# The signal's second stage on sums and differences of mirrored samples: a gated mix of a long convolution and an MLP

## The chip, the core and the metric

The kernel runs on one core of a Trainium2 chip. TensorE (PE) multiplies matrices, VectorE (DVE), ScalarE (ACT) and GpSimd (POOL) work on tiles in on-chip memory, SyncE (SP) mostly issues DMAs; ScalarE and GpSimd issue some too. Each engine runs its own instructions strictly in order and waits on semaphores for the others. The metric is the device time of one execution in microseconds (us). Everything is float32 (or fp32r, the same width).

## The reference

Rows of a signal u (2048 samples, 512 channels) are convolved with a kernel that a state-space model of 128 states gives for each channel; the same rows go through an MLP (512 to 1792 to 512, gelu); a gate per row mixes the two.

```python
P = exp(logdA[:, :, None] * l[None, None, :])       # 512 x 128 x 2048
K = einsum("dn,dnl,dn->dl", Cc, P, dB).real         # taps
y = irfft(rfft(pad(u)) * rfft(pad(K)))[:L] + u * Dskip
b = gelu(x @ w1 + b1) @ w2 + b2                     # x is u
g = sigmoid((x * gate_w).sum(-1))
out = g * y + (1 - g) * b
```

## The kernel before

Two functions follow one another: `front` and `conv`.

`front` computes the MLP, the taps K and the first stage of both Fourier transforms. Its work is cut into tasks by four streams (dense, taps, signal, early); each task has an engine, a hold (its modelled duration), a due time and dependencies, and the planner (`Plan.run`) gives out, engine by engine, the ready task with the earliest due time. The due times come from the constants at the file's head (T_, D_, W_). So these numbers set the order of every engine's instructions in the front. TensorE has three kinds of matmuls there: the hidden layer (ph, L917 to L919), the output layer (acc, L962 to L964) and the taps (pk, L726).

The transform of 4096 points is cut into two stages. In the **first stage** (`first_stage`, L428 to L442) 16 blocks of the signal (xl, 128 x 512 each, 256 KB) are multiplied, in four groups of 32 rows, with a small matrix c1t, two blocks (ux[0], ux[1]) per step, in eight steps; SP loads the blocks (L452), ScalarE copies the result out (L456), and SP stores it to memory (tu_d, L459). The stream `early` (L481) loads 27 of the 32 rows of tu_d again, 256 KB each, into the tiles den, attic and loft (`us[n]`). The taps go the same way: their first stage is stored to tk_d (L767).

MLP results are stored to `out` in memory and added to there: ScalarE copies acc into the tile io (L983), and GpSimd issues an accumulating store (L1006). The last two of these wait for `look` (L1014), a copy of one element on GpSimd that reads a tile xh after the last step of the hidden layer has written it (L937), so that all earlier traffic is through.

`conv` is written out by hand. It goes over 16 steps s of two rows each (n = 2s, 2s + 1), and in a step come:

- `fetch` of rows of tk_d for later steps (SP, L1129); the first N_TK = 8 are fetched ahead of the loop, with the matrices c2 (`consts`, L1121, 192 KB, cc) after every second one, four in all. The other matrices come at s = 2, 4, 6, 8. cc has four buffers in turn, tk has N_TK. Rows 16 to 23 go to t3 instead, at s = 0
- at s = 4, 5 and 6, loads of the five rows of tu_d that had no room in the front (SP, L1274)
- `product(s)`: six VectorE operations (L1174 to L1179) on the signal's spectrum (ur, ui in PSUM) and the taps' (kr, ki)
- `signal(s + 1)` and `taps(s + 2)`: the second stage (`pair`, L1152): for c = 0, 1 (real and imaginary part) and i = 0, 1 a matmul of a 128 x 64 matrix with a row tile of 128 x 512. For c = 0 the matrix is cut from cc (f), for c = 1 it is f1, whose halves are swapped and one negated (`matrices`: GpSimd for the first two, L1137 and L1138, ScalarE for the others, L1140 and L1141). ScalarE copies the taps' result out (L1160)
- `inverse(s)`: four matmuls with 64 x 64 matrices (pa, L1191), ScalarE copies (sa, L1197), SP stores to t_d (L1199); after each group of eight rows they are loaded again, turned, into t3 and den (`turn`, L1214). From s = 7 the MLP's results are loaded (L1228)

The profile counts a float32 matmul as two instructions: four matmuls of a group are x8. After the loop come `rest` (the last output-layer matmuls, L1245 to L1247), the last stage (pb, L1316), the gate and the stores (L1336).

Of the kernel before, what the change touches and what calls it, by code (L numbers as in the profile page):

```python
# [32 lines left out]
NB = 2 * NSB  # L33
T_0 = 28.031
T_MLP = 402.005
K_0 = 34.529
T_KG = 347.257
U_0 = 23
U_GAP = 18
LAG = 13.166  # L40
TABLE = 30.571
D_KA = -21.02
D_KP = -70.174
D_S1 = -64.005
D_EV = -0.687
D_H = -44.182
D_LO = -26.872
# [8 lines left out]
T_EARLY, T_LOFT, T_DEN = 434.731, 499.385, 583.061
Y_K, Y_U = 40.448, 33.741
W_MLP = (-0.0424, -0.0295, 0.0137)
W_KG = (-0.0358, -0.0266, -0.0229)
W_U = (-0.0255, -0.1355, -0.0209)  # L60
D_MAG = -1.089
D_ROT = 0.621
D_CON = -2.254
D_PHA = 0.57
D_PRE = -1.138
D_XL = 26
D_COE = -4.808
D_OUT = -10.383
D_DTB = -996.723
D_D0A = -269.982  # L70
D_LAST = -1.103
N_REST = 3
D_KA0 = 35
D_DT = 5
D_PRM = -94
D_D0 = 0
D_WAVE0 = -333.922
D_COE0 = -195.511
D_SP1 = -346.272
D_G0 = 14  # L80
D_GW = 568.694
D_XS0 = 115.71
T_PRE = 23
W_CAST = (0, 1, 0, 0, 1, 0, 1, 0, 1, 1, 0, 1, 0, 0)
X_CAST = (1, 1, 1, 1)
D_X0, D_B2, D_B2A, D_DM = -480, 20, -11.213, -79.268
N_G = 9

N_ATTIC, N_LOFT, N_TK = 11, 8, 8
ASIDE = (4, 6, 13, 14)  # L90
# [3 lines left out]
N_ROOM = N_ATTIC + N_LOFT  # L94
N_US = N_DEN + N_ROOM

# [35 lines left out]
def constants():  # L132


    def om(e4):
        a = 2.0 * np.pi * (np.asarray(e4) % (4 * L)) / (4 * L)
        return np.cos(a), -np.sin(a)

    k0 = np.arange(32)
    p = np.arange(32)  # L140
    q = np.asarray(slot_q())
    k1 = np.arange(64)
    m = np.arange(32)

    er, ei = om(4 * (64 * np.outer(p, k0) + 16 * p[:, None]))

    c1 = np.tile(np.stack([er, ei], 2).reshape(32, 64), (4, 1))


    ko = np.asarray(k0_order())  # L150
    turn = 2.0 * np.pi * (ko[:, None] + 0.25) / 32
    half = 2.0 * np.pi * (ko[:, None] + 0.25) / 64
    g1 = np.zeros((P, 2, 2, 32))
    for b in range(2):
        up, down = turn * (p - 1), turn * p
# [155 lines left out]
def gated_mix(  # L311
# [25 lines left out]
    tu_d = dr.tile([32, P, D], F32, name="tu_d")  # L337
    tk_d = dr.tile([32, P, D], F32, name="tk_d")

# [5 lines left out]
    gate = cp.tile([P, 2, 16], F32, name="gate")  # L345
    c1t = cp.tile([P, 64], F32, name="c1t")

    def places(attic, loft, den):

        rooms = [attic[:, k] for k in range(N_ATTIC)] + [loft[:, k * D : k * D + D] for k in range(N_LOFT)]  # L350
        return [den[:, k] for k in range(N_DEN)] + rooms + rooms[: 32 - N_US]

    def front(pool, psum, keep, attic, loft, den):

# [72 lines left out]

        def first_stage(xs, due, evac, ahead=2):  # L428

# [4 lines left out]
            def products():  # L434
                for r, (bank, _) in enumerate(banks):
                    rs = slice(32 * r, 32 * r + 32)
                    for m, (x, _) in enumerate(xs):
                        nc.tensor.matmul(bank[64 * m : 64 * m + 64], c1t[rs], x[rs], start=True, stop=True)  # L438

# [6 lines left out]
        def signal():  # L446
            for s in range(8):
# [3 lines left out]
                for m in range(2):  # L451
                    move(256, lambda m=m, s=s: nc.sync.dma_start(ux[m], xl[2 * s + m]), t - 10, [], [("ux", m)])  # L452

                def evac(r, pp, key, s=s, t=t):
                    k = take("st", N_ST)
                    act(512, lambda: nc.scalar.copy(st[k], pp), t + D_EV, [key], [("st", k)])  # L456
                    for m in range(2):
                        move(
                            128, lambda m=m: nc.sync.dma_start(rows[:, 8 * s + 4 * m + r], st[k][64 * m : 64 * m + 64]),  # L459
                            t, [("st", k)], [("u_d", 8 * s + 4 * m + r)], out=True,  # L460
                        )

                first_stage(xs, t, evac)
            yield None

        def early():

            us = places(attic, loft, den)
            keys = [("ux", 0)] + [("st", k) for k in range(N_ST)]
            keys = [*keys, *(("ld", k) for k in range(N_LD)), "gwb"]  # L470
            yield 1e6
            for n in range(N_US):
                m = n - N_DEN
                if m < 0:
                    due, key = T_DEN + n, [("xc", n // 4)]
                elif m < N_ATTIC:
                    due, key = T_EARLY + 2.5 * m, [keys[m]]
                else:
                    due, key = T_LOFT + m, ["xt", "xv"] if m < N_ATTIC + 4 else ["tt"]
                move(  # L480
# [235 lines left out]
        def contract(u, c, k, t):  # L716
# [382 lines left out]
        while heap:  # L1099
# [10 lines left out]
    def conv(pool, ps, late, attic, loft, den):  # L1110
# [4 lines left out]
        us = places(attic, loft, den)  # L1115
        ko = k0_order()
# [7 lines left out]
        def fetch(n):  # L1124
            if 16 <= n < 24:
                t2s[n] = t3[:, n]
            else:
                t2s[n] = pool.tile([P, D], F32, tag="tk", name=f"tk{n}", bufs=N_TK)
            nc.sync.dma_start(t2s[n], tk_d[ko[n]])  # L1129

        def matrices(m):
# [3 lines left out]
            f1 = pool.tile([P, 4, 64], F32, tag="f1", name=f"f1{m}", bufs=2)  # L1135
            if m < 2:
                nc.gpsimd.tensor_scalar(f1[0:64], f[64:128], -1.0, None, ALU.mult)  # L1137
                nc.gpsimd.tensor_copy(f1[64:128], f[0:64])  # L1138
            else:
                nc.scalar.mul(f1[0:64], f[64:128], -1.0)  # L1140
                nc.scalar.copy(f1[64:128], f[0:64])  # L1141
            mats[m] = (f, f1), cc[:, 256:384].rearrange("p (s k) -> p s k", s=2)
# [3 lines left out]
        def pair(s, r, c, out):  # L1146

            for i in range(2):
                n = 2 * s + i
                w = mats[n // 4][0][c][:, n % 4]  # L1150
                x = t2s[n] if r else us[n]
                nc.tensor.matmul(out[64 * i : 64 * i + 64], w, x, start=True, stop=True)  # L1152
# [110 lines left out]
        for s in range(16):  # L1263
# [92 lines left out]

# [65 lines left out]
```

## Time and profile before

| | us |
|---|---|
| three runs | 507.9, 507.18, 507.18 (median 507.18) |
| the profiled execution: its span | 506.3 |
| last hidden-layer matmul of the front begins | 398.03 |
| conv's first matmul begins | 398.24 |
| inverse(0) begins | 408.91 |
| pb begins (the last stage) | 487.04 |
| last VectorE operation begins | 501.05 |

The times are those of the runs; the profiled execution is another one, and all points inside it are counted from the start of its span. Differences are made against that span.

A group row reads: line, engine, operation, output<-input, shapes, count | busy us, mean ns of one | idle time of the engine just before, and what ended it. A row of a timeline or of the chain begins with its start and its duration in us. The chain is followed back from the last instruction: at each point stands what released the work that came next. `SPq` is SP's queue of issues.

### The profile page before, as it was taken

How to read it: one execution, taken by the hardware profiler on the slowest of the kernel's cores; microseconds unless marked ns; L12 is line 12 of the kernel's file. 1: busy time of each engine (PE TensorE's matmuls, PEld its weight loads, DVE VectorE, ACT ScalarE, POOL GpSimd, SP SyncE). 2: the span in 40 equal slices, each digit the busy share in tenths (PEclk: the TensorE clock that was granted, in tenths of full speed). 3: DMA queues.
4: the chain of work that ended last, by engine and by line, in shares of the span. 5: the costliest groups of instructions: out<-in, count | busy, mean ns of one | idle time of the engine just before them, and what ended most of it. 6: DMA issues, size and time to landing. Idle time of an engine off the chain costs nothing.

```text
span 506.3 us, 12185 instructions
## 1 busy us (share of the span) xinstructions
PE 494.8 (98%) x4798; PEld 380.3 (75%) x4798; DVE 429.0 (85%) x794; ACT 347.2 (69%) x625; POOL 53.5 (11%) x93
## 2 busy tenths in 40 slices
PE   7999999999999999999999999999999999999995
PEld 7886988998889889889789878989889722222551
DVE  6999999998999999999899989999921188877544
ACT  4898757699683889968487997657643445568513
POOL 1001010101002011011110012001010300020003
PEclk9999999999999999999999999999999999999998
DMA  8958896416788545889850276984588997999998
GB/s 288 381 178 235 298 296 219 84 65 200 182 239 222 156 147 126 262 187 238 201 128 2 84 167 156 208 266 104 189 208 180 282 390 266 336 374 382 320 321 312
DMA packets 82680, 112.32 MB, mean 222 GB/s; under 512 B 39644, under 2 KB 41184, under 8 KB 82080
## 3 DMA queue, kind: packets, MB, share of 16 engines
q1 hardware_dynamic: 74704, 87.06, 53.7%
q0 software_dynamic: 7264, 21.73, 18.3%
q10 hardware_dynamic: 656, 2.75, 1.7%
q8 instruction: 38, 0.62, 0.5%
q14 instruction: 18, 0.15, 0.1%
HBM read 61.71 MB, written 49.81 MB: 220 GB/s over the span
## 4 chain that ended last, share of the span: by engine, by line
PE 70%; DVE 13%; DMA 7%; ACT 4%; SPq 2%; issue 2%; DVEq 0%; ACTq 0%
PE pk L726 10%; PE acc L962 7%; PE ph L917 7%; PE ph L919 7%; PE ph L918 7%; PE acc L964 7%; PE acc L963 6%; PE p2u L1152 5%; PE p2k L1152 4%; PE pa L1191 3%; PE pb L1316 3%; DMA tk<-tk_d 2%; PE ph L438 2%; DVE y L689 2%; SPq L767 2%
## 5 line engine op out<-in xcount | busy, mean ns | idle before, releaser
L917 PE MATMUL ph<-xh,wh 128*128 128x256 f32 x448 | 127.7, 285 | 2.2 <-ACT wh L826 1.6
L919 PE MATMUL ph<-xh,wl 128*128 128x256 f32 x448 | 127.1, 284 | 0.4 <-DVE wl L828 0.4
L918 PE MATMUL ph<-xlo,wh 128*128 128x256 f32 x448 | 126.7, 283 | 0.0
L917 PEld LDWEIGHTS ph<-xh,wh 128*128 128x128 f32 x448 | 85.2, 190 | 9.5 <-issue 5.0
L918 PEld LDWEIGHTS ph<-xlo,wh 128*128 128x128 f32 x448 | 85.1, 190 | 1.8
L919 PEld LDWEIGHTS ph<-xh,wl 128*128 128x128 f32 x448 | 85.1, 190 | 1.0 <-DVE wl L828 1.0
L962 PE MATMUL acc<-wh,hh 128*128 128x512 f32 x206 | 83.2, 404 | 0.1
L964 PE MATMUL acc<-wh,hl 128*128 128x512 f32 x206 | 80.9, 393 | 0.5 <-DVE hl L947 0.5
L963 PE MATMUL acc<-wl,hh 128*128 128x512 f32 x206 | 80.9, 393 | 0.0
L934 ACT ACTIVATE ph<-ph,b1t 128x256 f32<-128x256 f32 x112 | 50.4, 450 | 43.6 <-PE ph L919 41.8
L726 PE MATMUL pk<-y,den 128*32 128x64 f32 x2048 | 61.4, 290 | 0.0
L726 PEld LDWEIGHTS pk<-y,den 128*32 128x32 f32 x2048 | 57.2, 136 | 3.5 <-issue 1.4
L962 PEld LDWEIGHTS acc<-wh,hh 128*128 128x128 f32 x206 | 38.7, 188 | 17.8 <-issue 7.4
L947 DVE TENSOR_TENSOR hl<-ph,hh 128x512 fp32r<-128x512 f32 (+1 forms) x62 | 38.4, 620 | 14.9 <-ACT hh L937 14.6
L689 DVE TENSOR_TENSOR y<-y,ea 128x64 f32<-128x64 f32 (+4 forms) x80 | 45.5, 569 | 2.1 <-ACT y L679 1.5
L964 PEld LDWEIGHTS acc<-wh,hl 128*128 128x128 f32 x206 | 38.7, 188 | 10.3 <-DVE hl L947 1.7
L963 PEld LDWEIGHTS acc<-wl,hh 128*128 128x128 f32 x206 | 38.7, 188 | 6.2
L937 ACT CAST hh<-ph 128x512 fp32r<-128x512 f32 (+1 forms) x62 | 33.0, 533 | 9.4 <-PE acc L963 6.2
L532 DVE TENSOR_TENSOR loft<-den,zz 128x256 f32<-128x256 f32 (+2 forms) x48 | 37.4, 779 | 0.7
L533 DVE TENSOR_TENSOR loft<-den,zz 128x256 f32<-128x256 f32 (+2 forms) x48 | 37.3, 777 | 0.0
L701 DVE TENSOR_TENSOR y<-y,loft 128x2048 f32<-128x2048 f32 x16 | 36.6, 2288 | 0.6 <-ACT loft L650 0.5
L1160 ACT COPY k<-p2k 128x512 f32<-128x512 f32 x32 | 18.5, 585 | 23.8 <-PE p2k L1152 8.0
(190 smaller groups left out, 876.0 us busy)
## 6 DMA issues: line engine op xcount, KB each, us to landing
tu_d<-attic SPq DMA_DIRECT2D x64, 128.0 KB, 3.9
tk_d<-sk SPq DMA_DIRECT2D x32, 256.0 KB, 5.3
t_d<-sa SPq DMA_DIRECT2D x32, 256.0 KB, 5.4
tk<-tk_d SPq DMA_DIRECT2D x24, 256.0 KB, 5.1
attic<-in_xt_dram SPq DMA_DIRECT2D x16, 256.0 KB, 5.1
xh_d<-xh SPq DMA_DIRECT2D x8, 512.0 KB, 5.0
xl_d<-xlo SPq DMA_DIRECT2D x8, 512.0 KB, 4.6
attic<-in_xs_dram SPq DMA_DIRECT2D x16, 256.0 KB, 4.9
```

Of the source, the lines that this page charges most:

```text
L532: vec(2 * m, lambda: vv.tensor_mul(t, a, br), due, [ka, *kb], [kt])
L689: nc.vector.tensor_mul(both(n, 64 - 3 * n, n), both(0, 64 - n, n), an)
L726: nc.tensor.matmul(pks[q][32 * j : 32 * j + 32, :, gg], x[:, r, :, ch], y[:, r, :, ch], start=(r == 0), stop=(r == 1), skip_group_check=True,)
L917: nc.tensor.matmul(p, h, xh[xk][:, d], start=(d == 0), stop=False)
L918: nc.tensor.matmul(p, h, xlo[xk][:, d], start=False, stop=False)
L919: nc.tensor.matmul(p, lo, xh[xk][:, d], start=False, stop=(d == 3))
L934: nc.scalar.activation(phs[q][:, n], phs[q][:, n], AF.Gelu_apprx_tanh, bias=b1t[:, f : f + 1])
L947: nc.vector.tensor_sub(lo, phs[q][:, 0:nf], hi.bitcast(F32))
L962: nc.tensor.matmul(a, h, wh[1][w], start=start, stop=False)
L963: nc.tensor.matmul(a, h, wl[1][w], start=False, stop=False)
L964: nc.tensor.matmul(a, l, wh[1][w], start=False, stop=(j == 3))
L1152: nc.tensor.matmul(out[64 * i : 64 * i + 64], w, x, start=True, stop=True)
```

## The change

The spectrum is wanted for real samples, so the second stage can take sums and differences of mirrored samples. The blocks of u are now paired so that block s and block 8 + s hold mirrored samples. For each signal step SP loads both, ScalarE multiplies the second by -1, and GpSimd issues two loads that add in the tile (`accum_op`): ux[0] becomes block s plus block 8 + s, ux[1] block s less block 8 + s. The first stage takes another matrix for ux[1] (c1t is 128 wide, with real and imaginary columns exchanged). A row tile of tu_d (128 x 512) then holds in its rows 0 to 63 the real parts of the sums and the imaginary parts of the differences, and in rows 64 to 127 the others; so the second stage needs, for c = 0, only the first 64 rows and, for c = 1, only the last 64, each with a 64 x 64 piece of cc.

`matrices` still makes f1, for the taps; since the rows of f stand in another order, its four pieces have 32 rows each, where there were two of 64. tk_d is laid out anew, [2, 32, 64, D], with the same bytes. All 32 rows of tu_d are loaded in the front: a new tile `shed` takes the last five, and the loads of L1274 go. N_TK becomes 9. The due times are taken from a table, DUE, of one number per task, in tenths of a microsecond; the constants have new values too. GpSimd's DMA scratch is given a size.

```diff
-T_0 = 28.031
+T_0 = 30.181
...
-N_ATTIC, N_LOFT, N_TK = 11, 8, 8
+N_ATTIC, N_LOFT, N_TK = 11, 8, 9
...
-N_US = N_DEN + N_ROOM
+
+DUE = (
+    -14012, -3058, -1619, -990, 254, -1062, 252, 2164, -206, -437, -438, -558, -1021, -1047, -3081, -2791, -3683,
...
+)
...
-    c1 = np.tile(np.stack([er, ei], 2).reshape(32, 64), (4, 1))
+    c1 = np.concatenate([np.stack(z, 2).reshape(32, 64) for z in ((er, ei), (ei, er))], 1)
+    c1 = np.tile(c1, (4, 1))
...
+    f2 = f2.reshape(32, 2, 2, 32, 64).transpose(0, 2, 1, 3, 4)
...
-    tk_d = dr.tile([32, P, D], F32, name="tk_d")
+    tk_d = dr.tile([2, 32, 64, D], F32, name="tk_d")
...
-    c1t = cp.tile([P, 64], F32, name="c1t")
+    c1t = cp.tile([P, 128], F32, name="c1t")
...
-        return [den[:, k] for k in range(N_DEN)] + rooms + rooms[: 32 - N_US]
+        return [den[:, k] for k in range(N_DEN)] + rooms + [shed[:, k] for k in range(32 - N_DEN - N_ROOM)]
...
-                        nc.tensor.matmul(bank[64 * m : 64 * m + 64], c1t[rs], x[rs], start=True, stop=True)
+                        w = c1t[rs, 64 * m * mirrored : 64 * m * mirrored + 64]
+                        nc.tensor.matmul(bank[64 * m : 64 * m + 64], w, x[rs], start=True, stop=True)
...
-                    move(256, lambda m=m, s=s: nc.sync.dma_start(ux[m], xl[2 * s + m]), t - 10, [], [("ux", m)])
+                    move(256, lambda m=m, s=s: nc.sync.dma_start(ux[m], xl[8 * m + s]), t + D_UL, [], [("ux", m)])
+                act(512, lambda: nc.scalar.mul(ux[1], ux[1], -1.0), t + D_UN, [], [("ux", 1)])
+                for m in range(2):
+                    move(
+                        540, lambda m=m, s=s: nc.gpsimd.dma_start(ux[m], xl[8 * (1 - m) + s], accum_op=ALU.add),
+                        t + D_UA, [], [("ux", m)], queue="GP", hold=0.8,
+                    )
...
-                            128, lambda m=m: nc.sync.dma_start(rows[:, 8 * s + 4 * m + r], st[k][64 * m : 64 * m + 64]),
-                            t, [("st", k)], [("u_d", 8 * s + 4 * m + r)], out=True,
+                            128, lambda m=m: nc.sync.dma_start(rows[:, 32 * m + 4 * s + r], st[k][64 * m : 64 * m + 64]),
+                            t, [("st", k)], [("u_d", 32 * m + 4 * s + r)], out=True,
...
-                first_stage(xs, t, evac)
+                first_stage(xs, t, evac, mirrored=1)
...
-            for n in range(N_US):
+            for n in range(32):
-                    due, key = T_LOFT + m, ["xt", "xv"] if m < N_ATTIC + 4 else ["tt"]
+                    due, key = T_LOFT + m, ["xt", "xv"] if m < N_ATTIC + 4 else ["tt"] if m < N_ROOM else []
...
+                sr = slice(h // 2 % 2 * 16, h // 2 % 2 * 16 + 16)
-                def store(n=n, ss=ss, d=d):
+                def store(h=h, n=n, ss=ss, sr=sr, d=d):
-                        tk_d[:, :, d : d + 64].rearrange("k (c s) g -> (k c) s g", c=2)[:, ss],
+                        tk_d[h // 4, :, :, d : d + 64].rearrange("k (c s) g -> (k c) s g", c=2)[:, sr],
...
+        for t, due in zip(pl.tasks, DUE, strict=True):
+            t.due = due / 10
...
-            nc.sync.dma_start(t2s[n], tk_d[ko[n]])
+            nc.sync.dma_start(t2s[n], tk_d[:, ko[n]])
-            if m < 2:
-                nc.gpsimd.tensor_scalar(f1[0:64], f[64:128], -1.0, None, ALU.mult)
-                nc.gpsimd.tensor_copy(f1[64:128], f[0:64])
-            else:
-                nc.scalar.mul(f1[0:64], f[64:128], -1.0)
-                nc.scalar.copy(f1[64:128], f[0:64])
+            for a in (0, 64):
+                re, im = slice(a, a + 32), slice(a + 32, a + 64)
+                if m < 2:
+                    nc.gpsimd.tensor_scalar(f1[re], f[im], -1.0, None, ALU.mult)
+                    nc.gpsimd.tensor_copy(f1[im], f[re])
+                else:
+                    nc.scalar.mul(f1[re], f[im], -1.0)
+                    nc.scalar.copy(f1[im], f[re])
...
-                w = mats[n // 4][0][c][:, n % 4]
-                x = t2s[n] if r else us[n]
+                if r:
+                    w, x = mats[n // 4][0][c][:, n % 4], t2s[n]
+                else:
+                    h = slice(64 * c, 64 * c + 64)
+                    w, x = mats[n // 4][0][0][h, n % 4], us[n][h]
...
                     fetch(n)
             if s in (2, 4, 6, 8):
                 consts(s // 2 + 3)
-            for n in range(2 * s + N_ROOM, min(2 * s + N_ROOM + 2, 32)) if s > 3 else ():
-                nc.sync.dma_start(us[n], tu_d[ko[n]])
             product(s)
             if s + 1 < 16:
                 signal(s + 1)
...
+    shed = keep.tile([P, 32 - N_DEN - N_ROOM, D], F32, name="shed")
...
-    nc = bacc.Bacc("TRN2", target_bir_lowering=False, num_devices=1)
+    nc = bacc.Bacc("TRN2", target_bir_lowering=False, num_devices=1, dynamic_dma_scratch_size=4096)
```

More of the change, by code (lines that the diff above doesn't have):

```diff
@@ L33 @@
 NB = 2 * NSB
-T_0 = 28.031
[L35 to L47, printed above, removed]
+T_0 = 30.181
+T_MLP = 394.707
+K_0 = 37.105
+T_KG = 355.412
+U_0 = 22.335
+U_GAP = 18.311
+LAG = 13.918
+TABLE = 32.374
+D_KA = -25.837
+D_KP = -7.351
+D_S1 = -39.706
+D_EV = -4.468
+D_H = -49.631
+D_LO = -47.233
 PS = (2, 3, 1, 2)
 N_ACC, N_H, N_PK, N_PU = PS
-D_SP = -0.459
+D_SP = 6.17
+D_UL, D_UN, D_UA = -26.734, -19.978, -26.418
 MEM = (6, 2, 3)
 N_LD, N_HL, N_ST = MEM
-D_XS = -150.061
+D_XS = -73.683
 D_G = 2.936
 N_WARM = 13
[L56 to L61, printed above, removed]
-D_ROT = 0.621
[L63 to L71, printed above, removed]
-N_REST = 3
[L73 to L84, printed above, removed]
+T_EARLY, T_LOFT, T_DEN = 268.769, 88.647, 688.804
+Y_K, Y_U = 39.373, 32.963
+W_MLP = (-0.0402, -0.0382, 0.0137)
+W_KG = (-0.0552, -0.0303, -0.0248)
+W_U = (-0.0299, -0.1355, -0.0182)
+D_MAG = -1.108
+D_ROT = 0.621
+D_CON = -2.853
+D_PHA = 0.521
+D_PRE = -0.43
+D_XL = -21.252
+D_COE = -12.806
+D_OUT = -43.76
+D_DTB = -1371.399
+D_D0A = -89.28
+D_LAST = 3.23
+N_REST = 3
+D_KA0 = 66.334
+D_DT = 3.379
+D_PRM = -94.216
+D_D0 = 19.524
+D_WAVE0 = -640.267
+D_COE0 = -98.47
+D_SP1 = -328.657
+D_G0 = -7.172
+D_GW = 807.205
+D_XS0 = 238.814
+T_PRE = 62.946
+W_CAST = (0, 0, 0, 1, 1, 0, 1, 0, 0, 1, 0, 1, 0, 0)
 X_CAST = (1, 1, 1, 1)
-D_X0, D_B2, D_B2A, D_DM = -480, 20, -11.213, -79.268
+D_X0, D_B2, D_B2A, D_DM = -252.638, 6.525, -2.867, 78.983
 N_G = 9
-N_ATTIC, N_LOFT, N_TK = 11, 8, 8
+N_ATTIC, N_LOFT, N_TK = 11, 8, 9
 ASIDE = (4, 6, 13, 14)
@@ L345, in gated_mix, with places, front @@
     gate = cp.tile([P, 2, 16], F32, name="gate")
-    c1t = cp.tile([P, 64], F32, name="c1t")
-    def places(attic, loft, den):
+    c1t = cp.tile([P, 128], F32, name="c1t")
+    def places(attic, loft, den, shed):
         rooms = [attic[:, k] for k in range(N_ATTIC)] + [loft[:, k * D : k * D + D] for k in range(N_LOFT)]
-        return [den[:, k] for k in range(N_DEN)] + rooms + rooms[: 32 - N_US]
-    def front(pool, psum, keep, attic, loft, den):
+        return [den[:, k] for k in range(N_DEN)] + rooms + [shed[:, k] for k in range(32 - N_DEN - N_ROOM)]
+    def front(pool, psum, keep, attic, loft, den, shed):
         pl = Plan()
@@ L426, in front, with first_stage @@
         step = [0]
-        def first_stage(xs, due, evac, ahead=2):
+        def first_stage(xs, due, evac, ahead=2, mirrored=0):
             q = (step[0] + ahead) % N_H
@@ L458, in evac @@
                         move(
-                            128, lambda m=m: nc.sync.dma_start(rows[:, 8 * s + 4 * m + r], st[k][64 * m : 64 * m + 64]),
-                            t, [("st", k)], [("u_d", 8 * s + 4 * m + r)], out=True,
+                            128, lambda m=m: nc.sync.dma_start(rows[:, 32 * m + 4 * s + r], st[k][64 * m : 64 * m + 64]),
+                            t, [("st", k)], [("u_d", 32 * m + 4 * s + r)], out=True,
                         )
-                first_stage(xs, t, evac)
+                first_stage(xs, t, evac, mirrored=1)
             yield None
         def early():
-            us = places(attic, loft, den)
+            us = places(attic, loft, den, shed)
             keys = [("ux", 0)] + [("st", k) for k in range(N_ST)]
@@ L1107, in front, with conv @@
         return sorted(late, key=lambda e: e[0])
-    def conv(pool, ps, late, attic, loft, den):
+    def conv(pool, ps, late, attic, loft, den, shed):
         sas = [pool.tile([P, D], F32, name=f"sa{k}", bufs=1) for k in range(6)]
         zs = [pool.tile([P, D], F32, name=f"z{k}", bufs=1) for k in range(2)]
-        us = places(attic, loft, den)
+        us = places(attic, loft, den, shed)
         ko = k0_order()
@@ L1349, in gated_mix @@
     ):
-        late = front(kp, ps, keep, attic, loft, den)
+        late = front(kp, ps, keep, attic, loft, den, shed)
     with (
@@ L1354, in gated_mix @@
     ):
-        conv(fp, ps_f, late, attic, loft, den)
+        conv(fp, ps_f, late, attic, loft, den, shed)
 _NAMES = [
```

87 rows, old and new, of the table DUE are left out of this document.

## The prediction

> **What bounds the kernel now.** First the page: the engine line, the slices and the shares of the chain.
>
> ```profile
> span 506.3 us, 12185 instructions
> PE 494.8 (98%) x4798; PEld 380.3 (75%) x4798; DVE 429.0 (85%) x794; ACT 347.2 (69%) x625; POOL 53.5 (11%) x93
> PE   7999999999999999999999999999999999999995
> DMA  8958896416788545889850276984588997999998
> PE 70%; DVE 13%; DMA 7%; ACT 4%; SPq 2%; issue 2%; DVEq 0%; ACTq 0%
> ```
>
> TensorE is busy throughout, so what shortens TensorE's work shortens the span, as far as nothing else steps in. In the last tenth the DMA digits are full too. The change shortens matmuls of conv, from 398 on; there the chain of waits, in order of time, reads:
>
> ```profile
> 408.91 1.69 PE pa L1191 x8
> 410.59 1.87 PE p2u L1152 x8
> 412.46 1.72 PE p2k L1152 x8
> 414.18 1.02 PE pa L1191 x8
> ...
> 469.42 1.02 PE pa L1191 x8
> 470.44 1.87 PE p2u L1152 x8
> ...
> 475.60 1.02 PE pa L1191 x8
> ...
> 487.04 13.91 PE pb L1316 x68
> ```
>
> Each step of conv is signal (p2u, 1.87), taps (p2k, 1.72) and inverse (pa, 1.02): 4.61 us, TensorE without a gap. From 410.59 to 470.44 there are 14 signals on the chain. Two other limits lie close, VectorE's products and the DMA engines:
>
> ```profile
> 406.37 0.69 DVE L1175 TENSOR_TENSOR v<-p2u,k 128x512 f32<-128x512 f32 x1 [1.95 <-DMA out_dram<-io]
> 406.98 0.68 DVE L1176 TENSOR_TENSOR z<-p2u,k 128x512 f32<-128x512 f32 x1
> DMA packets 13209, 29.54 MB, mean 340 GB/s; under 512 B 1520, under 2 KB 2372, under 8 KB 12741
> 400.00:420.00 20.00, 19.07 (x93) 6.95 (x90) 14.32 (x24) 8.48 (x17) 0.64 (x2) 1.00 1.05 356
> 412.00:416.00 4.00, 4.00 (x24) 0.99 (x21) 4.00 (x8) 1.92 (x4) 0.00 (x0) 1.00 1.05 394
> 420.00:440.00 20.00, 20.00 (x106) 5.59 (x104) 15.65 (x27) 11.54 (x22) 1.69 (x3) 1.00 0.83 283
> 440.00:460.00 20.00, 20.00 (x106) 5.41 (x102) 16.32 (x28) 12.38 (x23) 2.62 (x5) 1.00 1.01 376
> 464.00:468.00 4.00, 4.00 (x24) 1.02 (x22) 3.08 (x6) 3.64 (x7) 0.00 (x0) 1.00 1.06 408
> ```
>
> Six products, 0.60 apart (406.37 to 406.98), make 3.6 us a step. The DMA row is that of 400 to 487: 29.54 MB at 340 GB/s. The last two numbers of a window's row are the DMA share and GB/s: where the share is 1.0 or more, 356 to 408 were moved.
>
> **Term 1, the signal's matmuls.** TensorE's rows in one step of conv, before (cc holds the matrices, f the swapped ones, attic, loft and shed the signal's rows, tk the taps'):
>
> ```order
> L1152 MATMUL p2u_5324<-loft,cc_5082 64x512
> L1152 MATMUL p2u_5324<-attic,cc_5082 64x512
> L1152 MATMUL p2u_5327<-loft,f_5233 64x512
> L1152 MATMUL p2u_5327<-attic,f_5233 64x512
> L1152 MATMUL p2k_5330<-tk_5035,cc_5160 64x512
> ```
>
> TensorE at the same place in the change:
>
> ```order
> L1260 MATMUL p2u_5367<-loft,cc_5120 64x512
> L1260 MATMUL p2u_5367<-shed,cc_5120 64x512
> L1260 MATMUL p2u_5370<-loft,cc_5120 64x512
> L1260 MATMUL p2u_5370<-shed,cc_5120 64x512
> L1260 MATMUL p2k_5373<-tk_5037,cc_5199 64x512
> ```
>
> There are as many matmuls in the same place; each now takes 64 rows in instead of 128 and none needs f. That is the form of pa, the nearest row:
>
> ```profile
> L1191 PE MATMUL pa<-v,cc 64*64 64x512 f32 x128 | 18.0, 614 | 0.9 <-DVE v L1178 0.9
> L1152 PE MATMUL p2u<-attic,cc 128*64 128x512 f32 x32 | 9.7, 618 | 0.0
> ```
>
> One matmul lasts as long in both forms (614, 618 ns); four of 64x64 stand side by side, so the group of eight takes 1.02 and not 1.87. Switching between the two forms costs as often as before (once into taps, once out of them). The ends are 1.87 (four overlap no more than two did) and 1.02; I take pa's. **14 x 0.85 = 11.9 us off.** The new period is 3.76, still above VectorE's 3.6. In the last two steps, without taps, VectorE binds: inverse(13) to inverse(15) now takes 6.18 (469.42 to 475.60); with the shorter signal(15) it could be 5.33, but two products after signal(14) allow about 5.7: **+0.4**.
>
> **Term 2, conv's first product.** It waits for two accumulating stores:
>
> ```profile
> 391.21 1.08 ACT L983 COPY io<-acc 128x512 f32<-128x512 f32 x2
> 394.99 0.59 ACT L937 CAST xh<-ph 128x512 fp32r<-128x512 f32 x1
> 395.77 1.72 POOL L1006 DMA_DIRECT2D out_dram<-io  x2
> 400.01 1.29 PE L1152 MATMUL p2u<-den,cc 128*64 128x512 f32 x4
> 401.72 1.29 PE L1152 MATMUL p2k<-tk,cc 128*64 128x512 f32 x4
> 405.16 1.53 PE L1152 MATMUL p2k<-tk,cc 128*64 128x512 f32 x3
> 406.61 1.37 PE L1152 MATMUL p2k<-tk,f 128*64 128x512 f32 x3
> ```
>
> They go out at 395.77, after the cast at 394.99; DVE L1175 waits for them until 406.37 and inverse(0) starts at 408.91, though TensorE had finished its groups at 407.98 (406.61 + 1.37). ScalarE's rows at the end of the front, of before:
>
> ```order
> L937 CAST xh_105<-ph_87 128x512 [waits DMASW1_49,Activation_49]
> L983 COPY io_143<-acc_85 128x512 [waits DMASW7_49,PE_49]
> L983 COPY io_144<-acc_86 128x512 [waits DMASW0_49,PE_49]
> L934 ACTIVATE ph_88<-ph_88,b1t 128x256 [waits DVE_49,PE_49]
> L937 CAST xh_105<-ph_88 128x512 [waits Activation_49]
> ```
>
> ScalarE in the change:
>
> ```order
> L1038 CAST xh_106<-ph_89 128x512 [waits DMASW2_49,Activation_49]
> L1084 COPY io_144<-acc_86 128x512 [waits DMASW0_49,PE_49]
> L1084 COPY io_145<-acc_87 128x512 [waits DMASW7_49,PE_49]
> L1035 ACTIVATE ph_88<-ph_88,b1t 128x256 [waits PE_49]
> L1038 CAST xh_106<-ph_88 128x512 [waits Activation_49]
> ```
>
> The rows look alike, but the two columns of the hidden layer have changed places: the first element that POOL's look reads came from the second cast and now comes from the first, ahead of the io copies. So the stores go out once the copies end, 392.3 instead of 395.8: 3.5 us earlier. VectorE then has inverse(0)'s operand at about 405.4 (408.9 less 3.5). TensorE's own way from 400.01 is signal(0) 1.0 (now 1.71, to 401.72), taps 1.72, signal(1) 1.0, and taps(2), which now takes 2.82 (405.16 to 407.98) for want of a tk row: 406.7 with that wait, 405.6 without it. With pa's 1.02 behind it inverse(0) ends at 406.7 to 407.8 instead of 410.59: 2.8 to 3.9 off, and nothing if the stores land no earlier. I take **3.2 off**.
>
> **Term 3, SP's queue.** N_TK = 9 puts a fifth load of matrices into the prologue. SP's rows there, before (from tk6 on):
>
> ```order
> L1129 DMA tk_4781<-tk_d 128x512 [waits DMAHW3_49]
> L1129 DMA tk_4783<-tk_d 128x512 [waits DMAHW4_49]
> L1257 DMA g1t<-in_g_dram 128x128 [waits DMAHW5_49,PE_49]
> L1129 DMA tk_4818<-tk_d 128x512 [waits DMAHW6_49,PE_49]
> L1129 DMA tk_4820<-tk_d 128x512 [waits DMAHW7_49,PE_49]
> ```
>
> SP in the change, from tk7 on:
>
> ```order
> L1232 DMA tk_4813<-tk_d 128x1x512 [waits DMAHW1_49]
> L1224 DMA cc_4815<-in_c_dram 128x384 [waits DMAHW2_49,PE_49,Pool_49]
> L1232 DMA tk_4817<-tk_d 128x1x512 [waits DMAHW3_49]
> L1365 DMA g1t<-in_g_dram 128x128 [waits DMAHW4_49]
> L1232 DMA tk_4856<-tk_d 128x1x512 [waits DMAHW5_49]
> ```
>
> The ring of cc has four buffers, so the new cc load (it is read by nobody; cc4 is loaded again at step 2) waits until inverse(1), the last reader of cc0, is done. Behind it in SP stand tk8 to tk12, eight t loads and the first stores of sa. Before, tk8 waited only for taps(0).
>
> ```profile
> 392.10 0.38 SPq L1121 DMA_DIRECT2D cc<-in_c_dram  x1
> 393.19 0.80 SPq L1129 DMA_DIRECT2D tk<-tk_d  x2
> 400.09 0.33 SPq L1257 DMA_DIRECT2D g1t<-in_g_dram  x1
> DMA to landing us min/median/max: 3.0/5.1/9.8
> ```
>
> inverse(1) ends at 415.20 now, at 411.2 after terms 1 and 2 (less 3.2 and one signal). Then cc 0.38, tk8 0.40, g1t 0.33, tk9 0.40: tk9 is out at 412.7, and lands 3.0 (the least of the tk rows; the DMA engines stand nearly empty) to 5.1 later, 415.7 to 417.8. TensorE has signal(3) until 412.2 and then needs tk8 and tk9 for taps(4): it waits 3.5 to 5.6, nearer the lower end, **+4.0**. Had tk8 and tk9 landed before, it would cost nothing, but the queue is in order. In the gap VectorE gets a step ahead; nothing comes back, since TensorE is what is late next.
>
> **Term 4, the DMA engines.** TensorE alone would start pb at 487.0 - 11.9 - 3.2 + 4.0 + 0.4 = 476.3. To move until then: 29.54 MB, less five signal rows loaded earlier (1.31) and what goes out before SP is released (two accumulating stores, the last taps, some 1.5), plus 0.2 for the extra cc: 26.9 MB from 411.2 on, or 413 GB/s, more than any row shows. Gathers, stores and tk rows stand in one line for the same engines, so a backlog reaches TensorE through late taps or, at the end, through the last gathers, which pb needs. At 356, 376, 394 and 408 GB/s pb starts at 486.8, 482.7, 479.5 and 477.1. I take 480.0, near the two 4-us rows in the middle: **+3.7** (0 to +10.5).
>
> The Trainium skill ("DMA: Bandwidth & Descriptors", Specifications) gives an HBM limit of about 358 GB/s for a core and a fabric ceiling of 435. By 358 pb would start at 486.3, by 435 at 473.0, so that TensorE decides. The trace does not agree with the lower figure as a limit: 394 and 408 GB/s stand above it; the higher one no row reaches.
>
> **Term 5, the front.** Two rows bear on it, TensorE's and the others' busy time from 12 to 360 and the swap of a matrix on ScalarE:
>
> ```profile
> 12.00:360.00 348.00, 345.58 (x3875) 300.05 (x3874) 337.00 (x643) 271.57 (x487) 33.74 (x58) 1.00 0.66 184
> L1140 ACT ACTIVATE f<-cc x6: 415/415/416, 416.4 to 462.4; 64x256 f32<-64x256 f32 x6
> ```
>
> TensorE's work there stays. Added are 16 accumulating loads of 256 KB and eight ScalarE multiplications, off the chain as long as they come early; five signal rows are loaded there that were loaded in conv. The numbers of DUE put everything in a slightly other order. I take 0, with -2 to +3 from those few stalls that TensorE has there now (345.58 busy of 348) and as much again. The copies of f, four of 32 rows for two of 64, cost ScalarE 0.8 us more (two of 0.415) in each second step, hidden under its idle time (12.38 busy of 20): nothing. After pb's start nothing changes.
>
> **Sum.** 506.3 - 7.0 = 499.3 for the span; the median of the runs, 507.18, lies 0.9 above the profiled span, so **500.2 us** (the sum of the terms is -7.0).
>
> **Rivals.**
> - DMA does not bind: pb at 476.3, total 496.5. For it: the dense loads may come after pb's start. Against it: 413 GB/s. Chance 0.25; the forecast (497 to 504) has 0.46.
> - DMA carries on at the 356 GB/s of 400 to 420, where loads, stores and gathers were mixed: pb at 486.8, total 507.0, no change. Against it: 376 over 440 to 460. Chance 0.08. It is also what the lower figure of the Trainium skill above comes to.
> - The change does not shorten the signal's matmuls: the 64x64 ones overlap no more than two by two. Then term 1 and 1.4 of term 2 are lost and SP's stall stays: 507.2 + 4.0 - 1.8 = 509.4. Against it: pa's 1.02. Chance 0.05.
> - Slower, through POOL's queue in the front. POOL's rows in the front of the change, where the third signal step's accumulating loads (L550) stand ahead of the memset of y, from which VectorE's chain for the taps goes on:
>
> ```order
> L550 DMA attic<-in_xl_dram 128x512 [waits DMAHW1_49,DMASW2_49,PE_49]
> L550 DMA ux_103<-in_xl_dram 128x512 [waits DMASW3_49,PE_49,Activation_49]
> L778 MEMSET y 128x32 [waits PE_49,Pool_49]
> L1093 DMA out_dram<-b2b 128x512 [waits DMAHW6_49]
> L1093 DMA out_dram<-b2b 128x512 [waits DMAHW7_49,DMASW5_49]
> ```
>
> The first two are new there, and wait for a load, for ScalarE's multiplication and for TensorE's release of the tile.
>
> ```profile
> out_dram<-b2b POOLq DMA_DIRECT2D x16, 256.0 KB, 5.9
> ux<-in_xl_dram SPq DMA_DIRECT2D x8, 256.0 KB, 3.8
> L456 ACT COPY attic<-pu x16: 587/593/627, 41.7 to 326.9; 128x512 f32<-128x512 f32 x16
> L992 POOL DMA_DIRECT2D out_dram<-b2b x16: 832/854/1232, 42.0 to 220.8; - x16
> ```
>
> VectorE is busy 337.0 of 348 us from 12 to 360, so what it waits there it hardly makes good. A load (3.8), a multiplication (0.6, by the copy at L456), an issue (0.9) and an accumulation (5.9) make 11.2 us before a signal step's matmuls, where the load alone stood before. If the eight steps are due 1 us too early on average, 8 us are lost: 508.2, the point from which the change loses; at 2 us it is 516. Against it: POOL is busy for 11% of the span, so it can issue early. Chance 0.13; the last 0.03 go to a front that comes out better by more than 2.
>
> **Chances.** A measurement tells about 0.2% from no change. Faster: 0.46 + 0.25 + 0.03 = 0.74; within 0.2%: 0.08; slower: 0.05 + 0.13 = 0.18. The range takes in the case without a DMA bound with a front better by 2, the forecast, and no change: 494.5 to 507.5; outside it lie the two slower cases, 0.18, and the 0.03.
>
> **What would show it.** p2u groups of 1.02; SP's cc load waiting for inverse(1), and a gap of about 4 us before taps(4); inverse(0) some 6 us after conv's first p2u instead of 8.9; DMA windows at 380 to 408 GB/s from 412 to pb; pb's start 7 us earlier. It is wrong if that first p2u (400.01 now) comes later by more than 3 us, or if p2u stays at 1.7.

## The result and the profile after

| kernel | median, us | ratio to before, 95% interval |
|---|---|---|
| before | 507.54 | |
| changed | 655.65 | 1.292 (1.288 to 1.296) |

(To the three runs of before given ahead of the prediction a fourth has come, 508.26.) The change makes the kernel 29% slower; the forecast was 500.2, with a range up to 507.5. The page of the changed kernel, the engines, the slices, the DMA rate and the chain:

```profile
span 654.6 us, 12256 instructions
PE 519.6 (79%) x4798; PEld 382.0 (58%) x4798; DVE 429.9 (66%) x793; ACT 358.5 (55%) x647; POOL 70.1 (11%) x113
PE   8999999999999999999999996564530046356996
DMA  8996974579617996527779677111111223428998
GB/s 320 328 257 167 313 198 142 154 184 297 154 66 204 287 203 169 131 66 151 183 195 279 225 157 169 62 61 41 51 51 51 78 79 117 172 106 285 354 333 296
PE 56%; SPq 19%; DMA 12%; DVE 6%; ACT 3%; issue 3%; DVEq 0%; ACTq 0%
```

A slice is 16.4 us. Up to slice 24 (393 us) TensorE is full as before. Then its digits lie between 0 and 6 for thirteen slices, some 210 us, and those of the other engines no higher: none of them is the bound. The DMA digits say 1 for six slices and not 9, so one would not call it bound by DMA either; but the rate is remarkably even there, 41 to 62 GB/s and three times 51. And SP, which was 2% of the chain, is 19%. TensorE's waits, the longest first (us in total, times, longest), tell for what:

```profile
PE p2k L1260 <- DMA tk<-tk_d: 83.0, 12, 47.5
PE p2k L1260 <- issue: 19.0, 2, 11.0
...
```

Before, the same view has a single wait of 0.9 us from 397 to 480. It is the loads from tk_d that are late. SP's own timeline shows them (start, duration, issue; a duration is the time in which SP was held by its issues):

```profile
398.57 0.38 SPq L1224 DMA_DIRECT2D cc<-in_c_dram  x1
399.12 1.50 SPq L1232 DMA_DIRECT2D tk<-tk_d  x2
400.66 6.55 SPq L1224 DMA_DIRECT2D cc<-in_c_dram  x1
407.26 5.53 SPq L1232 DMA_DIRECT2D tk<-tk_d  x2
...
453.30 0.33 SPq L1224 DMA_DIRECT2D cc<-in_c_dram  x1
...
467.33 41.46 SPq L1232 DMA_DIRECT2D t<-tk_d  x8
508.90 7.79 SPq L1307 DMA_DIRECT2D t_d<-sa  x2
```

Before, the eight t loads read:

```profile
406.58 4.55 SPq L1129 DMA_DIRECT2D t<-tk_d  x8
```

They held SP for 4.55 us; here it is 41.46, that is 5.2 us for 256 KB, or 51 GB/s, the rate on the page. Loads of cc and stores of sa, which have kept their form, hold SP for 3 to 7 us each once they stand behind such loads. The windows from 460 to 500 and from 600 on, when the last tk load is through:

```profile
460.00:500.00 40.00, 14.20 (x50) 3.19 (x50) 7.37 (x12) 3.42 (x6) 0.00 (x0) 0.67 0.13 51
600.00:620.00 20.00, 18.90 (x102) 5.04 (x103) 12.74 (x21) 15.63 (x30) 3.14 (x6) 0.86 1.01 376
```

A DMA share of 0.13 is what two of 16 engines at full rate would make (0.125). A load that uses two engines at full rate looks, on a page of means, like idle DMA engines.

### The profile page after: what moved, and what is told of

Same layout as the page of the kernel before. It is cut to its first block, busy times and chain, and to the rows that moved or that the text cites. A ratio compares the mean times of both kernels' runs of the same rounds, so it can differ in the third digit from the quotient of the medians.

```text
span 654.6 us, 12256 instructions
## 1 busy us (share of the span) xinstructions
PE 519.6 (79%) x4798; PEld 382.0 (58%) x4798; DVE 429.9 (66%) x793; ACT 358.5 (55%) x647; POOL 70.1 (11%) x113
## 4 chain that ended last, share of the span: by engine, by line
PE 56%; SPq 19%; DMA 12%; DVE 6%; ACT 3%; issue 3%; DVEq 0%; ACTq 0%
SPq L1232 11%; PE pk L826 8%; PE ph L1018 7%; PE ph L1020 7%; PE ph L1019 7%; PE acc L1063 6%; PE acc L1064 6%; PE acc L1065 6%; DMA tk<-tk_d 4%; DMA t_d<-sa 4%; SPq L1224 4%; PE p2k L1260 2%; PE ph L532 2%; DMA cc<-in_c_dram 2%; PE pb L1422 2%
## 5 line engine op out<-in xcount | busy, mean ns | idle before, releaser
L1020 PE MATMUL ph<-xh,wl 128*128 128x256 f32 x448 | 127.0, 284 | 0.5 <-DVE wl L929 0.5
L1282 DVE TENSOR_TENSOR v<-p2u,k 128x512 f32<-128x512 f32 x16 | 11.1, 692 | 158.5 <-PE p2u L1260 142.0
L1260 PE MATMUL p2k<-tk,cc 128*64 128x512 f32 x48 | 29.3, 808 | 94.6 <-DMA tk<-tk_d 83.0
L1018 PEld LDWEIGHTS ph<-xh,wh 128*128 128x128 f32 x448 | 85.1, 190 | 12.8 <-issue 7.0
L1020 PEld LDWEIGHTS ph<-xh,wl 128*128 128x128 f32 x448 | 85.1, 190 | 0.9 <-DVE wl L929 0.9
L1260 PEld LDWEIGHTS p2k<-tk,cc 128*64 128x64 f32 x48 | 4.7, 165 | 114.9 <-DMA tk<-tk_d 81.9
L1305 ACT COPY sa<-pa 128x512 f32<-128x512 f32 x32 | 17.9, 589 | 88.3 <-DMA t_d<-sa 82.1
```

What stands on the lines that cost most here:

```text
L1018: nc.tensor.matmul(p, h, xh[xk][:, d], start=(d == 0), stop=False)
L1020: nc.tensor.matmul(p, lo, xh[xk][:, d], start=False, stop=(d == 3))
```

## The experiments

**First, the loads.** tk_d's new shape, [2, 32, 64, 512], makes the source of one load two blocks of 64 rows, 4 MB apart: three dimensions, 2 x 64 x 512, where there was one block of 128 rows. Theory A: a load runs on as many DMA engines as its outermost dimension can be dealt out to, here two. The rivals: something else in the change slows the queues (B), or SP's wait for inverse(1) does (C). split_loads:

```diff
-            nc.sync.dma_start(t2s[n], tk_d[:, ko[n]])
+            for e in range(2):
+                nc.sync.dma_start(t2s[n][64 * e : 64 * e + 64], tk_d[e, ko[n]])
```

> The changed kernel with each load from tk_d issued as two loads of 64 rows (64 x 512 each) instead of one whose outermost dimension is 2. Theory A (the new shape of tk_d puts each 256 KB load on 2 of the 16 DMA engines, 51 GB/s, 5.08 us, and everything behind it in SP's queue waits): DMA windows of conv go back to 280 to 408 GB/s, and the time comes to what the prediction had for conv, on a front that ends 4.8 us later: about 505, 499 to 509. Theory B (something else in the change slows the DMA queues: the accumulating loads or the smaller DMA scratch): still over 640. Theory C (SP's wait for inverse(1) in front of tk8 starves conv): still over 600, since that wait stays.

whole_rows:

```diff
-    tk_d = dr.tile([2, 32, 64, D], F32, name="tk_d")
+    tk_d = dr.tile([32, P, D], F32, name="tk_d")
...
-                        tk_d[h // 4, :, :, d : d + 64].rearrange("k (c s) g -> (k c) s g", c=2)[:, sr],
-                        sk[64 * n : 64 * n + 64, ss].rearrange("p s c j g -> p s (c j g)"),
+                    for e in range(2):
+                        r = 64 * (h // 4) + 32 * e + sr.start
...
+                            tk_d[:, r : r + 16, d : d + 64],
+                            sk[64 * n + e : 64 * n + 64 : 2, ss].rearrange("p s c j g -> p s (c j g)"),
...
-            nc.sync.dma_start(t2s[n], tk_d[:, ko[n]])
+            nc.sync.dma_start(t2s[n], tk_d[ko[n]])
```

> The changed kernel with tk_d back as [32, 128, 512], in the new order of rows; each load is one load of 128 rows again, and each store of the front is two stores of half the size. Theory A: 499 to 509 like the split loads, with half as many SP issues in conv (32 fewer of about 0.45 us), so 0 to 3 us less than those, or as much more if the 32 added stores delay the front. Theories B and C: over 600.

before_two_pieces, on the kernel before:

```diff
-            nc.sync.dma_start(t2s[n], tk_d[ko[n]])
+            nc.sync.dma_start(t2s[n], tk_d[ko[n] & 30 : (ko[n] & 30) + 2, 0:64])
```

> The kernel before, with each load from tk_d taking two blocks of 64 rows from two neighbouring rows of tk_d (an outermost dimension of 2 that cannot be merged), the same bytes; the taps are then the wrong ones. Nothing of the change is in it. Theory A: 32 loads of 5.08 us are 163 us of a queue that now needs under 60, so conv ends 90 to 150 us later: 600 to 660. Theories B and C: 507, no change.

before_scratch, on the kernel before:

```diff
-    nc = bacc.Bacc("TRN2", target_bir_lowering=False, num_devices=1)
+    nc = bacc.Bacc("TRN2", target_bir_lowering=False, num_devices=1, dynamic_dma_scratch_size=4096)
```

> The kernel before with the DMA scratch size of the change (4096). Theory A: 507, no change. Theory B in the form of the scratch: slower by tens of us.

| run | median, us | ratio to before, 95% interval |
|---|---|---|
| split_loads | 535.44 | 1.051 (1.045 to 1.057) |
| whole_rows | 521.0 | 1.026 (1.022 to 1.030) |
| before_two_pieces | 644.82 | 1.269 (1.264 to 1.274) |
| before_scratch | 507.37 | 0.999 (0.997 to 1.002) |

A stands, B and C fall as causes of the large loss: the load's form alone, in the kernel before, costs 138 us, and with whole rows (and each store of the front in two halves) the changed kernel loses 135 us of its excess. But both mended kernels miss their 499 to 509, so something more is wrong in both. And they lie 14 us apart, where 0 to 3 were expected: the split loads are twice as many issues (SP needs 10.23 us for the 16 t loads, 4.55 before), but from 420 to 440 they also move only 128 GB/s, at a share of 0.42. What makes the 14 us was not tried by itself. Theory A itself still had a rival: a source in separate blocks could be slow however many they are. So, with the same edit, four blocks of 32 rows (`ko[n] & 28`, 4, 0:32) and eight of 16 (`ko[n] & 24`, 8, 0:16):

> The kernel before, with each load from tk_d taking four blocks of 32 rows from four rows of tk_d (outermost dimension 4), the same bytes; the taps are the wrong ones. Theory A (a load runs on as many DMA engines as its outermost dimension has entries): 4 engines, about 102 GB/s, 2.5 us each, 82 us for the 32 loads instead of 163: 525 to 570, and windows of 100 GB/s at a DMA share of 0.25. Rival (a source in separate blocks is slow however many there are): 645 as with two.

> The same with eight blocks of 16 rows (outermost dimension 8). Theory A: 8 engines, 204 GB/s, 1.3 us each, 41 us for the 32 loads: 507 to 530. Rival: 645 or more.

Two, four and eight pieces took 644.82, 562.54 and 519.94 us. One window of each, in this order (that of eight lies within SP's t loads), and SP's issue of the eight t loads with four and eight:

```profile
440.00:450.00 10.00, 7.31 (x24) 1.72 (x24) 2.77 (x6) 3.06 (x6) 0.00 (x0) 0.83 0.13 50
```
```profile
420.00:430.00 10.00, 9.93 (x40) 2.66 (x40) 6.84 (x12) 4.72 (x9) 0.00 (x0) 1.00 0.26 100
```
```profile
410.00:414.00 4.00, 4.00 (x22) 1.00 (x22) 3.07 (x6) 2.24 (x4) 0.00 (x0) 1.00 0.53 200
```
```profile
422.38 21.14 SPq L1129 DMA_DIRECT2D t<-tk_d  x8
```
```profile
409.57 8.49 SPq L1129 DMA_DIRECT2D t<-tk_d  x8
```

The share is 0.13 with two blocks, 0.26 with four and 0.53 with eight; the rates are 50, 100 and 200 GB/s. All three fit one reading: each engine moves 25 GB/s, and the number of blocks is the number of engines. (16 times 25 is 400; the windows of before with a share of 1.05 and 1.06 moved 394 and 408.) So a source in separate blocks is not slow as such. SP is held for 5.2 us by a load in the changed kernel, for 2.6 with four blocks and 1.1 with eight; the last is less than the 1.3 of theory A, and traffic goes on at 205 GB/s from 418 to 420, after SP is through. The Trainium skill says so outright ("DMA: Bandwidth & Descriptors", Why a DMA increments its semaphore by 16 and not by 1): a DMA goes to the largest number of engines, 16 at most, that divides the slowest dimension other than 1 of both sides. For 2 against 128 that is two, for 4 four, for 8 eight, for 128 against 128 it is 16. The runs with two, four and eight blocks agree, to a few per cent in the rates.

**Second, what is left of whole_rows: 521.0, not 500.** Its chain from conv's start on, and TensorE's waits:

```profile
418.35 1.02 PE pa L1301 x8
419.37 0.86 PE p2u L1262 x8
...
422.09 1.11 PE pa L1301 x8
423.21 0.02 SPq L1226
...
433.96 5.17 DMA tk<-tk_d
```
```profile
PE p2k L1262 <- ACT f L1248: 6.6, 5, 2.5
PE p2k L1262 <- DMA tk<-tk_d: 6.3, 3, 3.2
```

The shape of the prediction is there: p2u now takes 0.86, and SP (L1226, the load of cc) starts when inverse(1) is through, TensorE waiting for tk rows behind it. A wait that the prediction had dismissed looks as large: the half-size copies of f on ScalarE. The single waits (in brackets) sort this out:

```profile
408.75 2.40 PE L1262 MATMUL p2k<-tk,cc 128*64 128x512 f32 x4 [3.24 <-DMA tk<-tk_d]
426.51 1.04 PE L1262 MATMUL p2k<-tk,cc 128*64 128x512 f32 x2 [2.54 <-ACT f L1248]
428.25 0.64 PE L1262 MATMUL p2k<-tk,cc 128*64 128x512 f32 x1 [0.70 <-DMA tk<-tk_d]
439.17 1.72 PE L1262 MATMUL p2k<-tk,cc 128*64 128x512 f32 x2 [2.37 <-DMA tk<-tk_d]
```

The first, 3.2 us, comes ahead of conv's first taps, before SP's stall. The second is put down to f, but this matmul does not read f, and that copy ended at 425.93; tk8, which SP issued at 423.64, is the likelier cause. Then SP's stall costs 2.5, 0.7 and 2.4, or 5.6 us, and the copies of f the remaining 4.1. no_early_cc takes the fifth load away from whole_rows, early_swap also makes the copies a step earlier:

```diff
-            if n % 2 == 0:
+            if n % 2 == 0 and n < 8:
                 consts(n // 2)
```

> The kernel with whole rows (521.0), without the fifth load of matrices in the prologue; cc4 is loaded at step 2 alone. Theory A (that load holds SP until inverse(1), and TensorE then waits for tk8 and tk9; the prediction had 4.0 for it, the profile of the whole rows shows TensorE idle for most of 425 to 439): 6 to 11 us less, 510 to 515. Rival (the DMA engines are busy there with what was issued anyhow, so that the rows land no earlier): 0 to 2 us less.

```diff
-            if s % 2 and s < 13:
+            if s % 2 == 0 and s < 12:
                 matrices(s // 2 + 2)
```

> no_early_cc with matrices(m) one step earlier, so that ScalarE's four half-size copies of f stand behind the copies of an earlier step. Theory A (the prediction took them as hidden, but TensorE waits 6.6 us for them in five places of the whole rows' profile): 4 to 7 us less than no_early_cc. Rival (ScalarE's sum of work sets the pace, or DMA does; the wait only moves to the copies of k): under 2 us less.

They took 515.25 us (1.014, 1.012 to 1.017) and 508.09 (1.001, 0.999 to 1.003): 5.75 for the load, a little less than expected and close to what the three waits make, and 7.2 for the copies, just above. A step of conv with and without the wait, in no_early_cc's timeline (the bracket is the idle time ahead):

```profile
421.73 1.09 PE L1301 MATMUL pa<-v,cc 64*64 64x512 f32 x8
...
425.69 1.08 PE L1262 MATMUL p2k<-tk,f 128*64 128x512 f32 x4 [1.01 <-ACT f L1248]
426.70 1.09 PE L1301 MATMUL pa<-v,cc 64*64 64x512 f32 x8
...
430.45 1.09 PE L1301 MATMUL pa<-v,cc 64*64 64x512 f32 x8
```

From inverse to inverse 4.97 us with the wait and 3.75 without; six such steps make 7.3 us. The copies fit into ScalarE's idle time, but they stood in its order right ahead of a matmul that needed them.

**Third, the terms by themselves**, both on early_swap. wide_signal puts the signal's stage back to 128 x 64; no_accumulation leaves out the 16 accumulating loads:

```diff
-                if r:
-                    w, x = mats[n // 4][0][c][:, n % 4], t2s[n]
-                else:
-                    h = slice(64 * c, 64 * c + 64)
-                    w, x = mats[n // 4][0][0][h, n % 4], us[n][h]
+                w, x = mats[n // 4][0][c][:, n % 4], t2s[n] if r else us[n]
```

> early_swap with the signal's second stage in the old form: 128 x 64 matrices on all 128 rows and f for c = 1; the values are then not the spectrum. Theory A (term 1: 0.85 us for each of 14 steps, with DMA not binding): 10 to 13 us more than early_swap. Rival (the DMA engines or VectorE bind conv by now, so that shorter matmuls are hardly worth anything): 0 to 5 us more.

```diff
-                        540, lambda m=m, s=s: nc.gpsimd.dma_start(ux[m], xl[8 * (1 - m) + s], accum_op=ALU.add),
+                        540, lambda: None,
```

> early_swap without the 16 accumulating loads in the front; the first stage then works on single samples and not on sums and differences. Theory A (the front's end is 4.8 to 7 us late because the accumulating loads hold up TensorE or take the DMA engines between 40 and 80 us): 4 to 7 us less than early_swap. Rival (the order that the table of due times makes is what is late, with or without them): under 1.5 us less.

wide_signal took 517.72 (1.021, 1.016 to 1.026): 9.6 more than early_swap, below the 10 to 13 but far from the rival's 5. Two inverses of it, and two of no_table below, which has the new form:

```profile
422.57 1.09 PE L1297 MATMUL pa<-v,cc 64*64 64x512 f32 x8
427.17 1.09 PE L1297 MATMUL pa<-v,cc 64*64 64x512 f32 x8
```
```profile
455.97 1.02 PE pa L1208 x8
456.99 0.86 PE p2u L1169 x8
...
459.72 1.02 PE pa L1208 x8
```

4.60 us a step against 3.75. no_accumulation took 507.07 (0.999, 0.996 to 1.001), about 1 us less than early_swap, within what these runs tell: theory A falls there. Its front ended late too (the last hidden matmul at 403.3), so not through the accumulating loads.

**Fourth, the front's order.** no_table takes the table away from early_swap, old_dues also sets the constants of the kernel before (with D_UL, D_UN, D_UA = -40, -32, -32):

```diff
-        for t, due in zip(pl.tasks, DUE, strict=True):
-            t.due = due / 10
```

> early_swap (508.1) without the table of due times; the due times come from the change's constants. Theory A (the front ends 4.8 to 7 us late because of the order that the table makes): the front's last hidden matmul comes back from 405 towards 398 and the time to 501 to 504. Rival (the front's lateness comes with the added work, whatever the order): 506 to 510, or more where the constants alone order it worse.

> early_swap without the table and with the constants of the kernel before; the signal's loads, multiplications and accumulating loads are due 40 and 32 us ahead of their step. Theory A: as no_table, the front's end at 398 to 400, and 500 to 503. Rival: the front's end stays at 403 or later.

no_table took 501.48 us (0.988, 0.984 to 0.992), 6.6 less than early_swap; old_dues took 508.33 (1.002, 1.000 to 1.004). The last hidden matmuls (L919, L1020, L931 and L931) in before, the changed kernel, no_table and old_dues; the two numbers behind the durations are the first and the last start:

```profile
L919 PE MATMUL ph<-xh,wl x448: 274/283/388, 8.2 to 398.0; 128*128 128x256 f32 x150
```
```profile
L1020 PE MATMUL ph<-xh,wl x448: 274/283/388, 7.9 to 402.9; 128*128 128x256 f32 x150
```
```profile
L931 PE MATMUL ph<-xh,wl x448: 276/283/387, 7.9 to 400.5; 128*128 128x256 f32 x150
```
```profile
L931 PE MATMUL ph<-xh,wl x448: 274/283/471, 8.1 to 406.7; 128*128 128x256 f32 x150
```

In these executions the table's order ends the front 4.9 us later than before, its constants alone 2.5, the old constants 8.7. But the last hidden matmul alone does not tell the kernels apart: it starts at 402.5 to 405.4 in six others with the table, and at 402.6 in no_table_late_gate (below), whose front is that of no_table. What differs clearly comes next. In every kernel with the table and mended loads TensorE waits 3.2 to 5.0 us for the tk row of conv's first taps, as here in late_gate (below); in no_table and no_table_late_gate it does not wait for it at all:

```profile
407.27 2.54 PE L1262 MATMUL p2k<-tk,cc 128*64 128x512 f32 x4 [3.61 <-DMA tk<-tk_d]
```
```profile
400.74 1.39 PE L1169 MATMUL p2k<-tk,cc 128*64 128x512 f32 x4
```

From 400.74 to 407.27 it is 6.5 us, about the 6.6 of the times. So no_table's time is the one that theory A gave, but only a part of it is the end of the hidden layer. old_dues misses its 500 to 503: there the rival holds. Which tasks of the table's order make that row late was not tried.

**Fifth, the end.** late_gate, on early_swap, moves ScalarE's multiplications of the dense halves two steps back (no_table_late_gate does it on no_table):

```diff
-            if s > 9:
-                gated(HERE[s - 10])
+            if s > 11:
+                gated(HERE[s - 12])
...
         dense(THERE[1], nc.scalar)
+        for k in HERE[4:]:
+            gated(k)
```

> early_swap with ScalarE's multiplications of the dense halves by the gate two steps later. Theory A (with the shorter steps the DMA engines come up to 12 us behind near the end; ScalarE stands waiting for a dense half and with it the copies of k and sa, so TensorE waits): 3 to 6 us less than early_swap. Rival (the last stores and gathers are late by themselves, so pb starts no earlier): under 1 us less.

> no_table (501.5) with the later multiplications of late_gate. Theory A (the DMA engines are near their limit, ScalarE's wait for a dense half costs TensorE about 1 us): 0.5 to 2 us less, 499.5 to 501. Rival (the gathers at the end set pb's start): no change, 501.5.

late_gate took 507.24 (1.000, 0.998 to 1.002), 0.9 less than early_swap, no_table_late_gate 502.85 (0.991, 0.989 to 0.993), 1.4 more than no_table: no gain that the runs can tell, and the rival stands. no_table is the fastest version, 1.2% (0.8 to 1.6) below before.

## Why the prediction was wrong

- **The step that failed** stands in term 3 and is taken over in term 4: a tk load "lands 3.0 (the least of the tk rows ...) to 5.1 later", and the DMA engines move 376 to 408 GB/s. Both are rows of before, for a load of another form. The new shape of tk_d, [2, 32, 64, D], was treated as the same bytes; that its load had another form stood in the rows that the prediction quotes (128x1x512 in place of 128x512). In its place the runs showed 5.2 us of SP for each such load, 51 GB/s, and everything behind it in SP's queue late. It cost 135 us (655.65 less 521.0), 138 by itself in the kernel before. The prediction's own sign of being wrong came with it: conv's first p2u starts at 419.31 instead of 400.01.
- **Term 1** was right: 0.85 a step was forecast, 4.60 less 3.75 measured; in the whole kernel 9.6 of the 11.9 (what took the other 2.3 was not tried).
- **Term 2** was right in kind; no run shows its 3.2. In the changed kernel the two accumulating stores go out at 397.42, 5.5 us ahead of the last hidden matmul; before it was 2.3 (395.77 to 398.0). That is 3.2 of the 3.5. In late_gate, with the same order and whole rows, VectorE's first product no longer waits for them, and inverse(0) starts 5.8 us after conv's first p2u (411.02 to 416.79; "some 6" was forecast, 8.9 before). But there the wait for the first tk row comes ahead of it. In no_table the stores go out only 3.0 us ahead of the last hidden matmul (397.48 to 400.53), and VectorE waits for them again, as the bracket of the second row shows.

```profile
397.42 1.72 POOL L1107 DMA_DIRECT2D out_dram<-io  x2 [1.03 <-ACT io L1084]
```
```profile
407.07 0.69 DVE L1191 TENSOR_TENSOR v<-p2u,k 128x512 f32<-128x512 f32 x1 [4.90 <-DMA out_dram<-io]
```

- **Term 3** was right as a mechanism: in the changed kernel SP's cc load at 453.30 follows the end of inverse(1) at 453.25. Its size, with whole rows, was 5.75 and not 4.0.

```profile
452.05 1.20 PE pa L1299 x8
```

- **Term 4** came out near in size, by chance. Without the bad loads (no_table) TensorE's own work would have brought pb 74.1 us after conv's first matmul (476.3 less the 4.0 of term 3, less 398.2); it came 77.4 after it (400.74 to 478.12), 3.3 late where 3.7 was forecast. But no steady limit of the DMA engines does that: conv's steps keep to 3.75 while 373 GB/s are moved (the DMA row below, from 411 to 478). The end takes 1.4 of it: pb starts 12.8 us after inverse(15), before 11.4 (475.60 to 487.04), and waits for a gather. The rest, 1.9, is at conv's start, in the place of term 2: inverse(1) starts 13.8 us after conv's first matmul (414.55), before 15.9 (398.24 to 414.18). The one shorter signal in between accounts for 0.85 of that gain, so 1.3 are left for term 2 and not 3.2. VectorE's wait for the stores (above) is one reason; weight loads of the taps wait there too, for ScalarE's copies of k (1.8 in all), for tk rows (0.9) and for POOL's pieces of f (0.8). How the 1.9 divide was not tried.

```profile
DMA packets 10684, 25.02 MB, mean 373 GB/s; under 512 B 1232, under 2 KB 1744, under 8 KB 10236
```
```profile
465.29 1.23 PE L1208 MATMUL pa<-v,cc 64*64 64x512 f32 x8
478.12 3.65 PE L1331 MATMUL pb<-den,g1t 128*64 128x512 f32 x16 [1.18 <-DMA den<-t_d]
```

- **Term 5** was wrong twice. The copies of f were costed at nothing because ScalarE is idle a third of the time; they cost 7.2, by their place. The front was costed at 0, up to 3; it ended 4.9 later, and with mended loads conv's first taps wait 3.2 to 5.0 for their row besides. Without the table the whole time is 6.6 less; the accumulating loads, on which the slower rival rested, account for 1 at most.
- None of the rivals was this one; the two slower ones rested on the signal's matmuls and on POOL's queue. That no_table's 501.48 is close to the forecast 500.2 is no merit of it: term 3's stall (4.0) and the swap's wait have been taken out there, and its front is 2.5 later (4.6 in no_table_late_gate).

## What to carry to other kernels

When a change alters the shape of a tensor in memory, read each load and store of it again as a list of dimensions: with an outermost dimension of 2 a 256 KB load took 5.2 us instead of the 0.64 that 408 GB/s make, and everything in the same queue waited with it. A DMA share that is small and even, like 0.13 at 51 GB/s, was here the sign of few engines and not of idle ones. An operation that fits into an engine's idle time costs nothing only if it also stands early enough in that engine's order.

## What the runs showed that was not expected

Loads that use two engines held up others, unchanged in form, in the same queue: the cc load held SP for 6.55 us behind two tk loads, and for 0.38 ahead of them. And TensorE worked more slowly after it had idled. In the changed kernel it begins only two matmuls between 455 and 467. The granted clock (the third number from the end of a window's row) is then 0.56, and an inverse takes 1.94 us; the next, 8.7 us later, finds a clock of 1.00 and takes 1.09:

```profile
470.89 1.94 PE L1299 MATMUL pa<-v,cc 64*64 64x512 f32 x8
...
479.57 1.09 PE L1299 MATMUL pa<-v,cc 64*64 64x512 f32 x8
```
```profile
470.00:473.00 3.00, 3.00 (x14) 0.71 (x16) 0.00 (x0) 0.68 (x2) 0.00 (x0) 0.56 0.13 51
479.00:482.00 3.00, 2.52 (x18) 0.51 (x16) 0.38 (x1) 1.03 (x2) 0.00 (x0) 1.00 0.13 51
```

So a stall cost somewhat more than its length here. That idling is what lowers the clock was not tried by itself.
